# Gate and value products of four token groups as seven half products, and attention numerators scaled in PSUM

## The chip, the core and the metric

The kernel runs on one core of a Trainium2 chip. A core has a matrix engine (TensorE, PE in the profile; its weight loads are shown as PEld), a vector engine (VectorE, DVE), a scalar engine (ScalarE, ACT), a general engine (GpSimd, POOL) and a sync engine (SP) that issues DMAs here. TensorE writes its results to PSUM, which this kernel uses as eight banks of 128 partitions x 512 fp32 values; ACT and DVE take them out; POOL works on SBUF alone in this kernel. Each engine runs its own instructions in the order of the program and waits on semaphores for the others. The metric is the device time of one execution in microseconds (us), lower is better.

## What is computed

A linear attention with an exponential feature map, followed by a gated feed-forward network (FFN):

```python
def phi(x):
    proj = np.einsum('bhsd,df->bhsf', x, w_phi)
    proj = proj - np.max(np.abs(proj), axis=-1, keepdims=True)
    return np.concatenate([np.exp(proj), np.exp(-proj)], axis=-1)
q_p, k_p = phi(q), phi(k)
kv  = np.einsum('bhsf,bhsd->bhfd', k_p, v);  z = np.sum(k_p, axis=2)
num = np.einsum('bhsf,bhfd->bhsd', q_p, kv)
den = np.einsum('bhsf,bhf->bhs', q_p, z)[..., None] + 1e-06
x   = (num / den)                      # to 4608 tokens x 512
out = (np.maximum(x @ w_gate, 0) * (x @ w_val)) @ w_out
```

There are 8 batches, 8 heads, 576 positions and a head size of 64; the FFN goes from 512 to 1536 and back to 512.

## The kernel before

**Tiles.** The first 512 positions of batch b form token group b (0 to 7), in four tiles of 128 tokens; the last 64 positions of all eight batches form group 8. A group's attention result, transposed, is `xT(g)`: four blocks of 128 rows (the 512 inputs of the FFN) by 512 tokens.

**Attention, numerators.** For each tile TensorE makes, per head, the product of the query features with the key-value sums for the two signs s of the exponential (`do_nu`, L899; 65 columns, of which the last is the denominator). The sum over the two signs has to be weighted: the s=1 part is multiplied by a factor per token and head (`cq`, or `cm` for group 8). The heads are taken in three parts of 2, 3 and 3 (`GROUPS`); a bank holds both signs of a part. VectorE then multiplies the s=1 part into an SBUF tile t (`do_nt`, L922), adds the s=0 part into u (`do_nv`, L932), takes the reciprocal of the denominators (`do_nr`, L942), and POOL multiplies u by it to the bf16 tile xu (`do_nx`, L954). A DMA transpose or TensorE turns xu into `xT`.

**FFN, first product.** `do_fv` and `do_fg` (through `ffn_in`, L1078) make a block of 128 of the 1536 value or gate columns for a group's 512 tokens: four matmuls of 128x512 that accumulate in one bank. The value block is copied out as bf16 `val` by ACT (`do_va`, L1096) or DVE (`do_vb`, L1099), and DVE makes h = max(gate, 0) * val (`do_ga`, L1102). Group 0 is done by 128-token tiles instead (L1110).

**FFN, second product.** Groups 1 to 8 already use a Strassen-like scheme (Winograd's form): h and `w_out` are cut in 2 x 2 blocks, and seven half products (`do_fw`, L1247, 12 matmuls of 256 columns each) take the place of eight. The sums of h blocks that it needs are made by POOL (`do_ps`) or DVE (`do_ds`), both L1223, 24 per group; the sums of weights once by POOL (`do_tw`, L1203). The partial results are put together on their way out: ACT copies two banks to SBUF (`do_ys`, L1272, and `do_y2`, L1275), and DVE adds to them in five more steps (`do_yw`, `do_yz`, `do_y1`, `do_y3`, `do_y4`, all L1278).

**Order.** Nothing is scheduled automatically. A string `ORDER` lists all steps (2239 words) in one sequence, each word with the step's name, its arguments, the PSUM banks after a colon and the ring buffers that it takes after an @. A step `x` calls `do_x`, which emits its instructions on their engines; so the sequence fixes each engine's order. Words `zz.n` are n dummy matmuls.

Of the kernel before, what the change touches and what calls it, by code (L numbers as in the profile page):

```python
# [28 lines left out]
vd.0.0.0:2@vs1 qz.0.0:3@my1 vs.0.1.1 qe.0.1.1.1:5 vp.0:2 qu.0.1@mz0 ke.0.2.1.0:6 qe.0.1.1.0:5 wl.0.0
vz.0:2 qb.0.2:4 zz.2:7 qb.1.3:3 zz.2:7 qb.1.2:1 vd.0.0.1:2 qu.0.0@mz1 vz.1:2 qe.0.1.3.0:3@qp2  # L30
vo.2@vs2 qw.0.0@cq0 qx.0.0.3:0 qx.0.0.2:4 qe.0.0.0.0:2 vs.0.2.1 zz.7:7 kv.0.0:6 qx.0.1.3:3 lw.1.1
vs.0.2.0 kc.0.0:6@kv0 kt.1.1@kT3 qe.0.0.0.1:2 kv.0.2:5 kv.0.1:6 qe.0.0.2.1:4@qp3 lm.1.1 kc.0.2:5
wl.1.1 kc.0.1:6 nu.0.0.0:2 nt.0.0.0:2@t0 zz.1:7 nu.0.0.2:5 qw.0.1 qx.0.1.2:1 qe.0.0.2.0:4
qe.0.1.3.1:3 nu.0.0.1:6 nv.0.0.0:2@u0 zz.2:7 nu.0.1.2:4 lv.1.2 nu.0.1.0:2 qe.0.1.2.1:1 nt.0.0.1:6@t1
lm.1.0 nt.0.0.2:5@t2 qy.0.2:3 nv.0.0.1:6 qe.0.0.3.0:0 nv.0.0.2:5 nt.0.1.0:2@t3 zz.2:7 nu.0.1.1:6
qy.0.3:5 nr.0.0@r0 qe.0.1.2.0:1 qz.0.2:3@my2 nv.0.1.0:2@u1 qz.0.3:5@my0 qu.0.2@mz2 zz.5:7
kr.1.1:3125 qe.0.0.3.1:0 nt.0.1.2:4@t0 nt.0.1.1:6@t1 qw.0.2 wl.1.0 nu.0.2.2:0 nx.0.0@xu0 nv.0.1.2:4
xp.0.0:7 nv.0.1.1:6 nt.0.2.2:0@t2 ke.1.1.3.1:5@kp3 nr.0.1@r1 nu.0.2.1:4 xa.0.0:7 nt.0.2.1:4@t3
nu.0.2.0:6 ke.1.1.0.1:3 nt.0.2.0:6@t0 qu.0.3@mz1 ke.1.1.0.0:3 pv.1.0:7 nv.0.2.1:4@u2 nv.0.2.2:0
nv.0.2.0:6 nu.0.3.1:4 qw.0.3 ke.1.1.1.0:1 nx.0.1@xu1 kx.1.1.0:3@mk3 xp.0.1:0 pa.1.0:7@val0  # L40
# [233 lines left out]
def kernel(  # L274
# [679 lines left out]
    def do_nx(bk, b, i):  # L954
        normalize(nc.gpsimd, b, i)
# [408 lines left out]
```

## Time and profile before

| what | value |
|---|---|
| device time, three runs | 366.55, 367.17, 368.11 us (median 367.17) |
| span of the profiled execution, first to last instruction | 365.2 us, granted TensorE clock 0.997 |
| instructions | 10031 |
| DMA traffic | 38.14 MB, mean 104 GB/s |

The profiled execution's own device time is not listed apart from its span; the median lies 1.97 us above that span. In the profile's lines a group of instructions is given as line, engine, operation, out<-in, shapes and count, then busy time in us and the mean of one in ns, then the idle time of the engine just before them with what ended it. In the timeline the columns are start in us, duration in us, engine, line and operation. A matmul's record includes its way through the array, so records of neighbours overlap.

### The profile page before, as it was taken

The numbers are of one execution on the slowest core, as the hardware profiler recorded it, in microseconds if no ns is written. First come the engines' busy times: TensorE is split into PE (matmuls) and PEld (weight loads), VectorE is DVE, ScalarE is ACT, GpSimd is POOL, SyncE is SP. The second block draws the span as 40 slices with busy tenths as digits, with TensorE's granted clock in tenths as the row PEclk, the third lists the DMA queues.
The fourth block names the chain that finished last, engine by engine and source line by source line (L and its number), as shares of the span: only waits on it lengthen the run. The fifth ranks groups of instructions, "written<-read, shape, count | busy, mean of one in ns | idle before, by whom it ended". The sixth has DMA issues, their size and how long they took to land.

```text
span 365.2 us, 10031 instructions
## 1 busy us (share of the span) xinstructions
PE 356.6 (98%) x3900; PEld 224.4 (61%) x3900; DVE 308.1 (84%) x723; ACT 228.8 (63%) x550; POOL 275.8 (76%) x337
## 2 busy tenths in 40 slices
PE   8999999999999999999999999999999999999993
PEld 6579865445575647755676456755457765545682
DVE  5999999989999998989988989899676945448872
ACT  4999996986698768695975278748854221121200
POOL 8765988999999999968997589946975793016600
PEclk9999999999999999999999999999999999999998
DMA  8999999983746893298219660397000320203016
GB/s 128 254 205 206 176 196 143 181 132 53 131 96 131 103 156 71 58 149 109 61 63 126 130 130 0 61 177 137 0 16 2 131 45 0 72 3 115 2 33 197
DMA packets 90768, 38.14 MB, mean 104 GB/s; under 512 B 64226, under 2 KB 86370, under 8 KB 90722
## 3 DMA queue, kind: packets, MB, share of 16 engines
q0 software_dynamic: 33504, 15.03, 32.5%
q1 hardware_dynamic: 56754, 21.83, 27.7%
q10 hardware_dynamic: 464, 0.66, 0.8%
q8 instruction: 30, 0.49, 0.6%
q14 instruction: 16, 0.13, 0.1%
HBM read 37.81 MB, written 9.44 MB: 129 GB/s over the span
## 4 chain that ended last, share of the span: by engine, by line
PE 81%; DVE 9%; POOL 4%; issue 2%; DMA 1%; ACT 1%; SPq 0%; DVEq 0%; POOLq 0%
PE bank L1081 42%; PE bank L1247 18%; PE bank L781 4%; PE bank L1110 4%; PE bank L904 3%; PE bank L1142 2%; PE bank L841 2%; PE bank L579 2%; POOL vs L1223 2%; DVE t L925 1%; DVE h L1102 1%; DVE u L935 1%; DMA w64f<-in_w_phi_dram 1%; ACT kp L675 1%; PE bank L442 1%
## 5 line engine op out<-in xcount | busy, mean ns | idle before, releaser
L675 ACT ACTIVATE kp<-bank 128x384 bf16<-128x384 f32 x192 | 84.1, 513 | 12.8 <-PE bank L579 6.0
L1081 PE MATMUL bank<-xTs,wv 128*128 128x512 bf16 x352 | 87.3, 379 | 0.0
L1096 ACT CAST val<-bank 128x512 bf16<-128x512 f32 x81 | 47.4, 592 | 62.8 <-PE bank L1081 55.7
L1081 PE MATMUL bank<-xTs,wg 128*128 128x512 bf16 x352 | 86.4, 379 | 0.0
L1102 DVE SCALAR_TENSOR_TENSOR h<-bank,val 128x512 bf16<-128x512 f32 x88 | 59.0, 681 | 22.1 <-PE bank L1081 15.0
L856 ACT ACTIVATE qp<-bank 128x512 bf16<-128x512 f32 x128 | 69.8, 619 | 5.3 <-PE bank L841 2.6
L1081 PEld LDWEIGHTS <-wg 128*128 128x128 bf16 x400 | 37.2, 98 | 41.0 <-issue 2.2
L1081 PEld LDWEIGHTS <-wv 128*128 128x128 bf16 x400 | 37.1, 98 | 38.0 <-DMA xTs<-xu 0.4
L732 POOL TENSOR_TENSOR vs<-vn,ek 128x780 bf16<-128x780 f32 (+2 forms) x40 | 53.9, 1364 | 1.2 <-ACT ek L692 0.7
L947 POOL TENSOR_TENSOR xu<-u,r 128x512 bf16<-128x512 f32 x36 | 37.3, 1044 | 16.8 <-DVE r L943 16.6
L683 DVE TENSOR_REDUCE mk<-bank 128x3 f32<-128x384 f32 x96 | 49.1, 542 | 1.0 <-ACT kp L675 0.9
L1247 PEld LDWEIGHTS <-h 128*128 128x128 bf16 x420 | 39.9, 98 | 9.5 <-issue 2.4
L1223 POOL TENSOR_TENSOR vs<-h 128x256 bf16<-128x256 bf16 x42 | 28.0, 670 | 21.4 <-DVE h L1102 14.4
L864 DVE TRANSPOSE_TENSOR_REDUCE maxq<-bank 128x16 f32<-128x512 f32 x56 | 37.1, 691 | 0.4 <-PE bank L841 0.2
L935 DVE TENSOR_TENSOR u<-bank,t 128x195 f32<-128x195 f32 (+1 forms) x108 | 32.7, 327 | 0.7
L925 DVE TENSOR_TENSOR t<-bank,cq 128x195 f32<-128x195 f32 (+1 forms) x96 | 29.4, 325 | 2.0 <-PE bank L904 1.7
L1247 PE MATMUL bank<-wo,h 128*128 128x256 bf16 x252 | 31.0, 273 | 0.0
L904 PEld LDWEIGHTS <-qp 128*128 128x128 bf16 x512 | 23.2, 98 | 10.8 <-issue 1.2
L1223 POOL TENSOR_TENSOR vs<-vs,h 128x256 bf16<-128x256 bf16 x42 | 27.9, 673 | 1.0 <-PE bank L1247 0.2
L904 PE MATMUL bank<-kv,qp 128*128 128x65 bf16 x512 | 26.1, 193 | 0.4 <-DVE u L935 0.2
L1223 POOL TENSOR_TENSOR h<-h 128x256 bf16<-128x256 bf16 x36 | 23.7, 670 | 0.3
L1223 POOL TENSOR_TENSOR h<-h,vs 128x256 bf16<-128x256 bf16 x36 | 23.7, 671 | 0.0
(134 smaller groups left out, 577.3 us busy)
## 6 DMA issues: line engine op xcount, KB each, us to landing
vn<-in_v_dram SPq DMA_DIRECT2D x24, 256.0 KB, 5.5
out_dram<-xTs SPq DMA_DIRECT2D x17, 256.0 KB, 2.4
kn<-in_k_dram POOLq DMA_DIRECT2D x7, 512.0 KB, 8.6
qn<-in_q_dram POOLq DMA_DIRECT2D x7, 512.0 KB, 8.0
out_dram<-obp SPq DMA_DIRECT2D x14, 256.0 KB, 2.4
wv<-in_moe_w_val_dram POOLq DMA_DIRECT2D x3, 512.0 KB, 8.9
wg<-in_moe_w_gate_dram POOLq DMA_DIRECT2D x3, 512.0 KB, 9.3
wo<-in_moe_w_out_dram POOLq DMA_DIRECT2D x3, 512.0 KB, 8.2
```

The source lines that it names most:

```text
L675: nc.scalar.activation(kp_of(3 * b + j)[:, i, s].rearrange("p n f -> p (n f)"), bank[bk[0]][:, 0 : 3 * F], AF.Exp, scale=(1.0, -1.0)[s],)
L683: nc.vector.tensor_reduce(mk_of(3 * b + j)[:, :, i], bank[bk[0]][:, 0 : 3 * F].rearrange("p (n f) -> p n f", f=F), axis=AX.X, op=ALU.max, ...
L732: nc.gpsimd.tensor_tensor(vs_of(3 * b + j)[:, s, 0:n].rearrange("p n i e -> p (n i) e")[:, :, 0:e], src[:, lo:hi].rearrange("p h i e -> p ...
L856: nc.scalar.activation(qp_of(4 * b + i)[:, s, 4 * hq : 4 * hq + 4].rearrange("p h m -> p (h m)"), bank[bk[0]], AF.Exp, scale=(1.0, -1.0)[s],)
L864: nc.vector.tensor_reduce((maxq0[:, i] if b == 0 else maxq)[:, :, i, 4 * hq : 4 * hq + 4].rearrange("p t h -> p h t"), bank[bk[0]].rearran ...
L904: nc.tensor.matmul(bank[bk[0]][:, E * n : E * (n + 1)], lhsT=qp_of(4 * b + i)[:, s, h, :], rhs=kv_of(b)[:, h, s, 0:E],)
L947: eng.tensor_tensor(xu_of(n).rearrange("p (h d) -> p h d", d=D), u_of(n)[:, :, 0:D], r_of(n).to_broadcast([P, H, D]), op=ALU.mult,)
L1081: nc.tensor.matmul(bank[bk[0]], lhsT=w[:, dc, P * f : P * f + P], rhs=xT(g)[:, dc, :], start=(dc == 0), stop=(dc == NDC - 1),)
L1096: nc.scalar.copy(val_of(NFC * g + f), bank[bk[0]])
L1102: nc.vector.scalar_tensor_tensor(h2_of(g, f), bank[bk[0]], 0.0, val_of(NFC * g + f), op0=ALU.max, op1=ALU.mult)
L1223: eng.tensor_tensor(sum_of(g, n, j), a, b, op=op)
L1247: nc.tensor.matmul(bank[bk[0]][:, col : col + HN], lhsT=x[:, P * u : P * (u + 1)], rhs=w, start=(n in (1, 5, 6) and u == us[0] and j == 0) ...
```

## The change

Four things change together.

**First product of groups 5, 6 and 8, 7.** They are taken in two pairs. The inputs (512) are cut in two halves, upper and lower; for a block f of 128 columns the four results wanted are gate and value of the first group of a pair and gate and value of the second. With x1, x2 the halves of the first group's `xT`, x3, x4 those of the second's, and G, V the gate and value weights (upper u, lower l), seven half products of two matmuls each (`do_fi`) are made:

```
S1 = Vu - Gu   S2 = Vl - S1   S3 = Vl - Vu   S4 = Gl - S2     (weights, once)
T1 = x3 + x4   T2 = T1 - x1   T3 = x1 - x3   T4 = x2 - T2     (tokens, per pair)
M1 = Gu x1   M2 = Gl x2   M3 = Vl T4   M4 = S4 x4   M5 = S1 T1   M6 = S2 T2   M7 = S3 T3
gate, first = M1+M2          value, first  = M1+M6+M5+M3
gate, second = M1+M6+M7+M4   value, second = M1+M6+M7+M5
```

The sums are seeded by copies: ACT copies the bank with M1 to a second bank (`do_ia`), M6 accumulates onto that copy, ACT copies the result to a third (`do_ib`), and M2, M7, M3 and M4 accumulate in place. M5 is copied to an SBUF tile qs by ACT (`do_iq`) or DVE (`do_ir`); DVE adds it to a bank to give the bf16 `val` (`do_iv`, twice per block), and M4 may only accumulate after the second of these has read its bank. `do_ga` is as before. The weight sums are 24 steps of 128x512 bf16 (22 on POOL, 2 on DVE), the token sums 16 (9 on POOL, 7 on DVE).

**Second product.** The same seeding takes the place of part of the adds: `do_fa` and `do_fb` copy one bank to another on ACT, later half products accumulate there, and fewer adds are left for DVE (15 of 128x512 and 2 of 128x256, against 38 and 4).

**Numerators.** The heads are taken in two halves of four. `do_nu` makes the s=1 part first; DVE multiplies it by the factor in place in PSUM (`do_nt`); a second `do_nu` accumulates the s=0 part on it; DVE takes the reciprocals from PSUM (`do_nr`, 4 columns) and writes xu from PSUM (`do_nx`). The tiles t and u and POOL's step are gone; TensorE's matmuls are as many as before.

**Order.** A new `ORDER` of 2386 words; 85 dummy matmuls as before. The number of buffers for h grows from 16 to 18, and group 6 and half of group 7 keep h in other tiles that are free by then.

```diff
-    GROUPS = HEADS
+    HALVES = ((0, 4), (4, 8))
...
     def do_nt(bk, b, i, g):
-        lo, hi = GROUPS[g]
-        n = hi - lo
+        lo, hi = HALVES[g]
         nc.vector.tensor_tensor(
-            t_of(3 * serial(b, i) + g)[:, 0:n],
-            parts(bk, n)[:, :, 1],
-            scales(b, i)[:, lo:hi][:, :, None].to_broadcast([P, n, E]),
+            part(bk, g),
+            part(bk, g),
+            scales(b, i)[:, lo:hi][:, :, None].to_broadcast([P, hi - lo, E]),
             op=ALU.mult,
         )
...
+    def do_fi(bk, p, f, n):
...
+        for dc in range(2):
+            nc.tensor.matmul(
+                bank[bk[0]],
+                lhsT=w[:, dc, P * f : P * f + P],
+                rhs=x[:, dc, :],
+                start=(n in (1, 5) and dc == 0),
+                stop=(dc == 1),
+                skip_group_check=(n not in (1, 5)),
+            )
+
+    def do_ia(bk, p, f):
+        nc.scalar.copy(bank[bk[1]], bank[bk[0]])
+
+    def do_ib(bk, p, f):
+        nc.scalar.copy(bank[bk[1]], bank[bk[0]])
+
+    def do_iq(bk, p, f):
+        nc.scalar.copy(qs_of(("in", p, f)), bank[bk[0]])
...
+    def do_iv(bk, p, f, u):
+        nc.vector.tensor_tensor(
+            val_of(NFC * PAIRS[p][u] + f), bank[bk[0]], qs_of(("in", p, f)), op=ALU.add
+        )
...
+    def do_fa(bk, g):
+        nc.scalar.copy(bank[bk[1]], bank[bk[0]])
```

The new order moves work on every engine; three places show what the prediction speaks of.

VectorE, numerators of group 4, before (lines of `before`: L925 is t, L935 is u, L943 the reciprocal, L1102 makes h):

```order
L925 TENSOR_TENSOR t_126<-bank_66,cq_115 128x195
L935 TENSOR_TENSOR u_127<-bank_66,t_126 128x195
L925 TENSOR_TENSOR t_123<-bank_67,cq_115 128x195
L935 TENSOR_TENSOR u_127<-bank_67,t_123 128x195
L1102 SCALAR_TENSOR_TENSOR h_152<-bank_68,val_143 128x512
L925 TENSOR_TENSOR t_125<-bank_69,cq_115 128x130
```

and now (L949 scales in place, L958 the reciprocal, L962 writes xu, L1000 and L1101 are a transpose and h):

```order
L949 TENSOR_TENSOR bank_66<-bank_66,cq_115 128x260
L949 TENSOR_TENSOR bank_69<-bank_69,cq_115 128x260
L1000 STREAM_TRANSPOSE qt_130<-qm_74 128x256
L1101 SCALAR_TENSOR_TENSOR h_148<-bank_70,val_137 128x512
L958 RECIPROCAL r_124<-bank_69 128x4
L958 RECIPROCAL r_123<-bank_66 128x4
L962 TENSOR_TENSOR xu_128<-bank_66,r_123 128x256
L962 TENSOR_TENSOR xu_126<-bank_69,r_124 128x256
```

Three pairs of steps per tile have become two triples, and between the first and the second of a triple TensorE has a part to add.

TensorE, block 5 of the second pair (groups 8 and 7), now; bank0 receives M1 of block 5, and bank5 is the copy of it that M6 accumulates on (xTm is `xT(8)`, the tiles kp, qT, qr and vn hold sums of weights and tokens):

```order
L1180 MATMUL bank0_63<-xTm_147,wg_143 128x512
L1180 LDWEIGHTS kp_2_83
L1180 MATMUL bank7_70<-xTs_146,kp_2_83 128x512
L1180 LDWEIGHTS kp_2_83
L1180 MATMUL bank7_70<-xTs_146,kp_2_83 128x512
L1180 LDWEIGHTS wv_144
L1180 MATMUL bank2_65<-qr_0_131,wv_144 128x512
L1180 LDWEIGHTS wv_144
L1180 MATMUL bank2_65<-qr_0_131,wv_144 128x512
L1180 LDWEIGHTS kp_0_81
L1180 MATMUL bank5_68<-qT_0_107,kp_0_81 128x512
```

Two half products of other blocks (bank7 and bank2) stand between the product that is copied and the one that needs the copy; before, no TensorE instruction of the FFN's first product needed anything of ACT or DVE beyond `xT` and a free bank.

SP, the end of its queue, before (L1304, L1308 and L1300 write results of groups 8, 7 and 7):

```order
L1304 DMA out_dram<-obp 64x512 x2
L1308 DMA out_dram<-xTs 128x2x256
L1304 DMA out_dram<-obp 64x512 x2
L1308 DMA out_dram<-xTs 128x2x256 x2
L1300 DMA out_dram<-xTs 128x256
```

and now (L1429, L1421 and L1425 write results of groups 7, 7 and 8):

```order
L1429 DMA out_dram<-xTs 128x2x256 x2
L1421 DMA out_dram<-xTs 128x256
L1425 DMA out_dram<-obp 64x512 x4
```

Four DMAs of group 8's half tiles, which wait for the last half product of all, have become the last of the queue; before, it was one DMA.

743 lines of the change are left out of this document (414 added, 329 removed).

## Prediction

> **What bounds the kernel now.** I read the page's first part, then busy time by stretch, then the chain that ended last, then who waited for whom.
>
> ```profile
> PE 356.6 (98%) x3900; PEld 224.4 (61%) x3900; DVE 308.1 (84%) x723; ACT 228.8 (63%) x550; POOL 275.8 (76%) x337
> ```
>
> ```profile
> 0.00:220.00 220.00, 217.36 (x2687) 138.18 (x2688) 206.30 (x501) 171.28 (x423) 193.60 (x230) 1.00 0.84 132
> 220.00:300.00 80.00, 79.99 (x841) 49.70 (x840) 62.99 (x151) 47.77 (x111) 63.63 (x81) 1.00 0.35 65
> 300.00:360.00 60.00, 59.23 (x376) 36.49 (x373) 38.85 (x72) 9.75 (x18) 18.57 (x28) 1.00 0.17 50
> ```
>
> The columns are the stretch, its length, busy time of PE, PEld, DVE, ACT and POOL, the granted clock, the DMA share and GB/s. PE is never free after the start. VectorE is at 94% up to 220 us and has 17.0 + 21.2 = 38.2 us free after that.
>
> A busy PE might hide waits, since records overlap; the chain and the waits tell:
>
> ```profile
> PE 81%; DVE 9%; POOL 4%; issue 2%; DMA 1%; ACT 1%; SPq 0%; DVEq 0%; POOLq 0%
> ```
>
> ```profile
> 316.71 13.81 PE bank L1081 x64
> 331.84 10.36 PE bank L1081 x48
> 342.20 17.05 PE bank L1247 x156
> ```
>
> ```profile
> PE bank L904 <- DVE u L935: 0.2, 1, 0.2
> PE bank L904 <- ACT kv L792: 0.2, 1, 0.2
> PE bank L1247 <- DVE obp L1278: 0.2, 1, 0.2
> ```
>
> Matmuls of the first product follow one another at 13.81/64 = 0.216 us, those of the second at 17.05/156 = 0.109 us, and after the start nothing holds PE for more than 0.2 us at a time. So PE's own work sets the time, and taking PE work away pays in full unless a wait comes in its place.
>
> **The change, part by part.**
>
> *PE.* A pair's block took 2 groups x 2 products x 4 = 16 matmuls and now takes 7 x 2 = 14. Over 2 pairs x 12 blocks that is 48 matmuls of 128x512 fewer: 48 x 0.216 = **-10.4 us**. The numerators keep their matmuls (16 of 65 columns a tile, now in two visits), and so does the second product.
>
> *VectorE.* The rows:
>
> ```profile
> L1102 DVE SCALAR_TENSOR_TENSOR h<-bank,val 128x512 bf16<-128x512 f32 x88 | 59.0, 681 | 22.1 <-PE bank L1081 15.0 <-ACT val L1096 5.1 <-PE bank L1247 1.1
> L935 DVE TENSOR_TENSOR u<-bank,t 128x195 f32<-128x195 f32 x72 | 24.3, 352 | 0.7
> L925 DVE TENSOR_TENSOR t<-bank,cq 128x195 f32<-128x195 f32 x64 | 21.4, 345 | 1.3 <-PE bank L904 1.1
> L935 DVE TENSOR_TENSOR u<-bank,t 128x130 f32<-128x130 f32 x36 | 10.0, 278 | 0.1
> L1278 DVE TENSOR_TENSOR obp<-bank,obp 128x512 f32<-128x512 f32 x21 | 14.2, 681 | 4.3 <-PE bank L1247 4.3
> L1278 DVE TENSOR_TENSOR xTs<-bank,xTs 128x256 f32<-128x256 f32 x4 | 1.7, 424 | 0.3 <-PE bank L1247 0.2
> L943 DVE RECIPROCAL r<-u 128x8 f32<-128x8 f32 x36 | 6.6, 189 | 0.2
> L1223 DVE TENSOR_TENSOR kp<-kp 128x256 bf16<-128x256 bf16 x6 | 3.1, 515 | 0.0
> L1223 DVE TENSOR_TENSOR kp<-kp,vs 128x256 bf16<-128x256 bf16 x6 | 1.6, 281 | 0.0
> ```
>
> A tile's numerator took 2 x (0.345 + 0.352) + 2 x 0.28 + 0.19 = 2.14 us of VectorE. Now it takes two steps that scale in place, two that write xu, and two reciprocals. No row shows VectorE writing to PSUM. From below the bound is the 195-column row, 0.345; from above a whole bank, 0.681. A step of 256 columns that reads PSUM takes 0.424, and I take 0.42 for both: 2 x (0.42 + 0.42 + 0.19) = 2.06, or 36 x 0.08 = 3 us less in all. Then 48 adds that make val: + 48 x 0.68 = 32.7; M5 copied by VectorE 7 times: + 4.8; 18 value copies fewer: - 12.3 (the whole-bank price); the second product's adds, 23 of 0.68 and 2 of 0.42 fewer and 5 copies more: - 13.1; 20 sums of h more, at 0.28 to 0.52, say 0.43: + 8.6; 9 sums of 128x512, bounded by 0.28 and twice 0.52, say 0.55: + 5. Together about +23, so 331 us of busy time in a span near 357, or 93%.
>
> Does this fit? The numerators keep the stretch to 220 us as full as it is. The first products of groups 5 to 8 come after that, where 38 us are free and some 32 us (32.7 + 4.8 + 8.6 + 5 - half of 12.3 - half of 13.1) are added, while the stretch loses 10 us. By records it is just too much. But records overlap in a dense queue:
>
> ```profile
> 327.98 1.29 DVE L1102 SCALAR_TENSOR_TENSOR h<-bank,val 128x512 bf16<-128x512 f32 x2 [1.66 <-PE bank L1081]
> ```
>
> Two whole-bank steps of 0.69 take 1.29, so the second starts 0.60 after the first. A block of a pair needs 2 adds and 2 h steps, 4 x 0.60 = 2.4 us, in the 14 x 0.216 = 3.0 us that PE spends on it. VectorE stays behind PE's work, with some 15% to spare in the densest stage.
>
> *ScalarE.* It gains 63 whole copies from bank to bank, 2 halves, and 23 copies to qs, and loses 30 value copies and 3 others:
>
> ```profile
> L1096 ACT CAST val<-bank 128x512 bf16<-128x512 f32 x81 | 47.4, 592 | 62.8 <-PE bank L1081 55.7 <-DVE h L1102 5.2 <-DVE u L935 0.6
> L1151 ACT COPY obp<-bank 128x512 f32<-128x512 f32 x2 | 1.3, 673 | 0.0
> L703 ACT ACTIVATE bank<-mk 128x12 f32<-128x12 f32 x2 | 0.4, 180 | 0.0
> ```
>
> At 0.59 this is +33 us, 262 of 357: no bound by itself. What matters is the delay of a copy, because PE now waits for it. From the end of the chain of matmuls:
>
> ```profile
> 352.51 1.47 PE L1247 MATMUL bank<-kp,kp 128*128 128x256 bf16 x12
> 353.82 0.82 PE L1247 MATMUL bank<-wo,vs 128*128 128x256 bf16 x6
> 354.02 1.22 DVE L1278 TENSOR_TENSOR xTs<-bank,xTs 128x512 f32<-128x512 f32 x2 [0.42 <-PE bank L1247]
> ```
>
> PE was free at 353.82, and the reader of its bank started at 354.02: 0.20 us. With the same 0.04 between the record's end (353.98) and the reader taken for the way back, a seed costs 0.20 + 0.59 + 0.04 = 0.83 us from PE to PE. Counted in the new order at the rows' prices, the nearest use of a seed stands two half products later, 4 x 0.216 = 0.86, in 10 of 48 places, and 0.79 in one; the rest have 0.98 or more. So at the row's price it is covered, and the queue on ACT has to be free at that moment. The in-place step has 0.20 + 0.42 + 0.04 = 0.66; six of the 72 parts have less than that between their two visits (0.39 to 0.59), which is 1.0 us in sum. Bounds for all these waits: nothing, and 4.1 us for a seed of 1.15 (a copy of 0.91). I take **+1.0 us**. The two small rows on a bank of 12 columns let me expect no dearer copy: L703, which writes PSUM, has 0.18. The Trainium skill's "PSUM — Partial Sum Buffer" (Specifications, the engine access table) says that ScalarE writes faster to PSUM than to SBUF; by that a seed would be below 0.83 and the sum 0.1 us less, and no row here shows it for a whole bank.
>
> *POOL.* It loses 36 steps of 1.04 and 26 sums of 0.67, and gains 31 sums of 128x512:
>
> ```profile
> L947 POOL TENSOR_TENSOR xu<-u,r 128x512 bf16<-128x512 f32 x36 | 37.3, 1044 | 16.8 <-DVE r L943 16.6
> L1223 POOL TENSOR_TENSOR vs<-h 128x256 bf16<-128x256 bf16 x42 | 28.0, 670 | 21.4 <-DVE h L1102 14.4 <-PE bank L781 5.3 <-DMA xTm<-xu 1.5
> L1203 POOL TENSOR_TENSOR kp<-wo 128x768 bf16<-128x768 bf16 x4 | 6.6, 1647 | 0.0
> ```
>
> Half way between 0.67 and 1.65 is 1.16; 31 of them make 36 us, so the total falls by some 19 us to 257. But 22 weight sums (25 us) stand close together behind the last key scaling of group 7, because they use tiles that only then are free, and the first pair needs them third by third. PE's first pair takes 36 us for its 12 blocks, and the first third is needed at once. Bounds: hidden, and 4 of these sums late, 4.6 us. I take **+0.5 us**, near the lower end, since the order puts PE's work on group 7's queries and numerators in front.
>
> *The end.*
>
> ```profile
> 357.75 1.47 PE L1247 MATMUL bank<-wo,kp 128*128 128x256 bf16 x12
> 359.64 0.94 ACTq L1323 DMA_DIRECT2D out_dram<-xTs  x1
> 359.71 0.34 SPq L1300 DMA_DIRECT2D out_dram<-xTs  x1
> 355.32 1.15 SPq L1304 DMA_DIRECT2D out_dram<-obp  x2
> out_dram<-xTs ACTq DMA_DIRECT2D x1, 128.0 KB, 4.6
> out_dram<-obp SPq DMA_DIRECT2D x4, 128.0 KB, 2.4
> ```
>
> PE is free at 359.06 (12 x 0.109 after 357.75), the last DMA starts 0.65 later and lands after 4.6, behind others. Now a whole-bank copy comes after the last matmul (0.20 + 0.59 + 0.05 = 0.84), and four DMAs at 1.15/2 = 0.58 each, so the last starts at 2.6. If it lands after 2.4 the end comes 0.2 us earlier than before; after 4.6, 2.0 us later. I take the middle, **+0.9 us**.
>
> *Sum.* 365.2 - 10.4 + 1.0 + 0.5 + 0.9 = 357.2 us of span. The profiled execution's span is 1.97 below the median of the runs shown (367.17), so the forecast is **359.2 us**; by the parts' own bounds 356.9 (no waits, landing after 2.4) to 367.
>
> **The rivals.**
>
> *VectorE in bursts: 364.* 331 us of records and the 10 us that it cannot use (the start, and the last 6 us) leave 16 of 357. If the sums of h share their time with POOL's (0.52 against 0.28 in two rows of one shape) and val comes late, PE waits for a bank. 44 sums x 0.12 more is 5 us. For it speaks the 94% up to 220 us; against it that PE hardly waits there now.
>
> *The in-place step costs two passes, slower: 373.* One mechanism: reading and writing one bank, VectorE takes as long as for t and u together, 0.83 us for 260 columns, by the two rows of 195. That adds 72 x 0.41 = 30, so VectorE needs 361 + 10, and the span ends at 371. The point from which it decides is 16/72 = 0.22 more than 0.42, so 0.64 us. Nothing here shows a VectorE write to PSUM; against it speaks that t and u take the same for different outputs.
>
> *Seeds are slow: 369.* A bank-to-bank copy of twice 0.59 makes a seed of 1.42; 29 of the 48 places have 1.31 or less behind them, and what they lack sums to 10 us. That is the gain given back. For it: no row shows a whole-bank copy into PSUM; against it: the rows of ACT's whole-bank copies lie between 0.59 and 0.67 whatever they write.
>
> *POOL's weight sums are late: 363,* by the 4.6 above.
>
> *The clock falls: 366.* PE would stop briefly at many seeds, and a lower clock would double its steps, as at the start:
>
> ```profile
> 1.06 3.38 PE L442 MATMUL bank<-zero 128*128 128x256 bf16 x15 [1.06 <-DVE zero L428]
> 15.51 0.94 PE L442 MATMUL bank<-zero 128*128 128x256 bf16 x7
> ```
>
> (3.38 - 0.42)/14 = 0.21 us each there, (0.94 - 0.27)/6 = 0.11 later. If a tenth of the 336 half-product matmuls ran so, 34 x 0.216 = 7 us. Against it: the clock stands at 1.00 in all three stretches. The Trainium skill's "TensorE: Matmul & The Clock Gate" (A second HAM failure mode: psum-queue depth-cycling) speaks for this rival: it reports a kernel that cycled through PSUM banks at 512 columns and whose short idles between groups made the clock go down and up. This trace, with eight banks in turn and no such idles, does not show it.
>
> **How the numbers follow.** Chances: the forecast 0.62, VectorE in bursts 0.09, POOL late 0.08, two passes 0.13, slow seeds 0.05, clock 0.03. About 0.5%, 1.8 us, is what a measurement of this kernel can tell from no change. Faster takes the forecast, the two late cases: 0.79; same takes the slow seeds and the clock: 0.08; slower takes the two passes: 0.13. The range leaves out the two passes and the worst of the seeds above, and little below: 355.5 to 368; the forecast's own range is 356.5 to 362.
>
> **What would show it.** Right: some 48 fewer matmuls of 128x512, PE's records without gaps to the end, PE's first and last matmul about 10 us closer, VectorE near 330 us, clock 1.00. Each step: L949 at about 0.42 (over 0.64 is the slower case); bank-to-bank copies near 0.59 (1.18 is the slow seed); waits of PE on DVE in the numerators, on ACT and POOL in the half products of the first product; the last copy at 0.8 and the last DMA 2.6 us after PE's end. It is wrong if PE shows waits of over 5 us in sum, whoever is named.

## The result and the profile after

The changed kernel takes 387.45 us (median of five runs, 383.83 to 393.64), the kernel before 367.20 (366.55 to 368.11) beside it: a ratio of 1.053, 95% interval 1.0475 to 1.0587. One of the five runs, 393.64, is in a slower state, and the ratio is that of the other four. The kernel is slower by 20 us where 8 us less were forecast. The profiled execution took 389.48 us, with a span of 387.7 us.

The page of the changed kernel, engines, clock in 40 slices, and the chain that ended last:

```profile
PE 359.4 (93%) x3852; PEld 225.8 (58%) x3852; DVE 339.0 (87%) x736; ACT 254.8 (66%) x608; POOL 259.6 (67%) x306
PEclk9988899999999998799999999999999999999998
PE 58%; POOL 13%; DVE 12%; DMA 8%; SPq 3%; issue 2%; ACT 1%; POOLq 0%; DVEq 0%; ACTq 0%
```

The 48 matmuls are gone (3900 to 3852). But TensorE's share of the chain fell from 81% to 58%, that of POOL rose from 4% to 13%, that of the DMAs from 1% to 8% and that of SP's queue from 0 to 3%, and the clock sags in slices 3 to 5 and in 16 and 17.

Busy time by stretch (columns as in the prediction), first the kernel before, then the changed one:

```profile
0.00:60.00 60.00, 57.84 (x862) 42.88 (x866) 55.62 (x143) 50.90 (x130) 47.24 (x61) 1.00 1.19 189
100.00:160.00 60.00, 59.73 (x727) 38.43 (x724) 57.21 (x133) 48.53 (x120) 57.62 (x70) 1.00 0.59 106
240.00:280.00 40.00, 39.99 (x330) 21.78 (x327) 31.62 (x68) 26.85 (x63) 28.87 (x35) 1.00 0.40 67
```

```profile
0.00:60.00 60.00, 52.13 (x710) 40.51 (x711) 47.16 (x108) 43.75 (x107) 34.80 (x47) 0.91 1.15 185
100.00:160.00 60.00, 51.07 (x544) 29.57 (x541) 48.71 (x105) 42.48 (x106) 43.99 (x51) 0.91 0.61 101
240.00:280.00 40.00, 37.58 (x461) 23.51 (x459) 39.80 (x94) 28.90 (x69) 39.13 (x40) 1.00 0.21 48
```

In the first two stretches every engine is busy less, VectorE too, at 0.91 of the clock (POOL also has the 36 steps to xu less to do). When all engines idle more, either a load is late or the engines wait for each other in turn; the waits have to tell which. Neither stretch holds a pair's first product, which starts at 262.4 us, but both hold the new numerators. The waits of the changed kernel (us in total, times, longest):

```profile
POOL vr L782 <- DMA vm<-in_v_dram: 16.6, 2, 12.6
PEld L1210 <- DMA wg<-in_moe_w_gate_dram: 3.0, 1, 3.0
PE bank L803 <- POOL vs L754: 4.3, 2, 3.7
PE bank L1347 <- DVE vs L1323: 5.1, 2, 3.6
PE bank L1180 <- DVE qT L1152: 1.2, 1, 1.2
PE bank L1180 <- POOL kp L1125: 0.5, 1, 0.5
ACT bank L1190 <- PE bank L1180: 13.9, 11, 2.9
```

All waits of PE that the profile lists add up to 21.8 us, after 2.4 in the kernel before, and before, no step of POOL waits for vm. By the prediction's own sign (over 5 us of such waits) it is wrong.

The largest loss can be followed through three timelines (start, duration, engine, line), of SP's queue, of POOL, of PE:

```profile
130.95 8.06 SPq L540 DMA_DIRECT2D vn<-in_v_dram  x4
139.06 4.18 SPq L1421 DMA_DIRECT2D out_dram<-obp  x1
143.28 0.63 SPq L559 DMA_DIRECT2D vm<-in_v_dram  x1
```

```profile
133.78 0.94 POOL L505 DMA_DIRECT2D qn<-in_q_dram  x1
147.34 1.05 POOL L782 TENSOR_TENSOR vr<-vm,ek 64x520 bf16<-64x520 f32 x1 [12.61 <-DMA vm<-in_v_dram]
149.13 1.50 POOL L754 TENSOR_TENSOR vs<-vn,ek 128x780 bf16<-128x780 f32 x1
```

```profile
152.70 0.38 PE L803 MATMUL bank<-vs,kp 128*128 128x65 bf16 x4 [3.69 <-POOL vs L754]
```

In the new order the small load of batch 4 (the last 64 rows of v, 64 KB, tile vm) stands on SP's queue behind the four loads of vn and an output. The five took 12.2 us to issue. POOL's next step reads vm, so POOL stood for 12.6 us; the scalings of the values behind it were late, and PE waited for them, with a lower clock after it.

Another stop of PE, of nearly the same size, has VectorE's name. At 110.92 us VectorE began a sum of h that took 4.29 us, while POOL ran its own steps one behind the other:

```profile
110.92 4.29 DVE L1323 TENSOR_TENSOR vs<-h 128x256 bf16<-128x256 bf16 x1
115.28 2.53 PE L1347 MATMUL bank<-wo,vs 128*128 128x256 bf16 x11 [3.58 <-DVE vs L1323]
```

All other sums of this shape take 0.28 to 1.13 us. POOL had come to this place after a wait of 4.0 us for batch 3's vm, at 98 to 102. In e2_vm below, where only loads of vm move, the same sum takes 0.46 us and this wait of PE is gone. So late loads can stand behind a wait that names an engine; why the sum took so long at this place is not shown.

To see what each stretch lost I took, for every matmul of the trace, the time to the start of the next, less what its kind takes where nothing holds it (the lower quartile of its kind after 60 us in the two first traces); dummy matmuls count as loss. Matmuls that a later trace lacks (45) are put in at their kind's price. This is worked out, not a view of the profile. PE's work at undisturbed prices is 314.4 us before and 304.0 us after, 10.4 less. PE's loss:

| stretch, us | before | changed | e3_both | e6_v4 | e13_v2 | e14_light | e16_order |
|---|---|---|---|---|---|---|---|
| 0 to 60 | 20.3 | 29.5 | 25.6 | 25.3 | 23.3 | 23.3 | 29.2 |
| 60 to 100 | 5.0 | 5.2 | 5.0 | 5.0 | 5.3 | 5.3 | 5.1 |
| 100 to 160 | 7.5 | 19.3 | 15.2 | 11.5 | 10.3 | 9.7 | 20.0 |
| 160 to 240 | 7.3 | 9.0 | 9.0 | 9.4 | 10.7 | 9.9 | 8.5 |
| 240 to 280 | 3.1 | 9.6 | 7.6 | 6.7 | 5.9 | 3.3 | 6.9 |
| 280 to end | 0.9 | 4.2 | 4.2 | 4.2 | 4.1 | 3.9 | 4.1 |
| sum | 44.1 | 76.9 | 66.7 | 62.2 | 59.7 | 55.3 | 73.9 |

So -10.4 of work and +32.8 of loss make the +22.4 of span. 21 of the 32.8 lie in the stretches 0 to 60 and 100 to 160.

### The profile page after: what moved, and what is told of

Its sections match the earlier page's. It is cut to its first block, busy times and chain, and to the rows that moved or that the text cites. A ratio compares the mean times of both kernels' runs of the same rounds, so it can differ in the third digit from the quotient of the medians.

```text
span 387.7 us, 10020 instructions
## 1 busy us (share of the span) xinstructions
PE 359.4 (93%) x3852; PEld 225.8 (58%) x3852; DVE 339.0 (87%) x736; ACT 254.8 (66%) x608; POOL 259.6 (67%) x306
## 3 DMA queue, kind: packets, MB, share of 16 engines
q0 software_dynamic: 33504, 15.03, 29.8%
## 4 chain that ended last, share of the span: by engine, by line
PE 58%; POOL 13%; DVE 12%; DMA 8%; SPq 3%; issue 2%; ACT 1%; POOLq 0%; DVEq 0%; ACTq 0%
PE bank L1080 15%; PE bank L1180 14%; PE bank L1347 9%; DMA wg<-in_moe_w_gate_dram 4%; PE bank L1210 4%; POOL vs L754 3%; PE bank L803 3%; DMA vm<-in_v_dram 3%; PE bank L1242 3%; PE bank L464 2%; PE bank L925 2%; DVE vs L1323 2%; SPq L540 2%; PE bank L601 2%; POOL vs L1323 2%
## 5 line engine op out<-in xcount | busy, mean ns | idle before, releaser
L1101 DVE SCALAR_TENSOR_TENSOR h<-bank,val 128x512 bf16<-128x512 f32 x82 | 55.2, 678 | 4.5 <-PE bank L1080 2.7
L754 POOL TENSOR_TENSOR vs<-vn,ek 128x780 bf16<-128x780 f32 (+2 forms) x40 | 54.0, 1360 | 3.1 <-ACT ek L714 2.7
L1080 PE MATMUL bank<-xTs,wv 128*128 128x512 bf16 x208 | 53.2, 389 | 0.0
L1080 PE MATMUL bank<-xTs,wg 128*128 128x512 bf16 x208 | 52.0, 382 | 0.9 <-DVE h L1101 0.9
L1323 POOL TENSOR_TENSOR vs<-h 128x256 bf16<-128x256 bf16 x31 | 20.6, 669 | 43.6 <-DVE h L1101 43.0
L1347 PEld LDWEIGHTS <-h 128*128 128x128 bf16 x396 | 38.0, 98 | 8.2 <-DVE h L1323 0.9
L1095 ACT CAST val<-bank 128x512 bf16<-128x512 f32 x51 | 30.5, 619 | 13.7 <-PE bank L1080 12.0
L1202 DVE TENSOR_TENSOR val<-bank,qs 128x512 bf16<-128x512 f32 x48 | 31.8, 680 | 7.9 <-PE bank L1180 4.7
L925 PEld LDWEIGHTS <-qp 128*128 128x128 bf16 x512 | 25.7, 100 | 14.4 <-issue 3.0
L782 POOL TENSOR_TENSOR vr<-vm,ek 64x520 bf16<-64x520 f32 x14 | 14.8, 1055 | 25.2 <-DMA vm<-in_v_dram 16.6
L1080 PEld LDWEIGHTS <-wg 128*128 128x128 bf16 x208 | 18.4, 98 | 21.4 <-issue 4.7
L1080 PEld LDWEIGHTS <-wv 128*128 128x128 bf16 x208 | 19.1, 99 | 19.8 <-issue 2.3
L1347 PE MATMUL bank<-wo,h 128*128 128x256 bf16 x240 | 29.7, 274 | 0.3 <-DVE h L1323 0.3
L925 PE MATMUL bank<-kv,qp 128*128 128x65 bf16 x512 | 29.1, 197 | 0.8 <-ACT kv L814 0.6
L949 DVE TENSOR_TENSOR bank<-bank,cq 128x260 f32<-128x260 f32 x64 | 25.9, 424 | 4.1 <-PE bank L925 4.0
L962 DVE TENSOR_TENSOR xu<-bank,r 128x256 bf16<-128x256 f32 x72 | 28.1, 410 | 0.2
L1190 ACT COPY bank<-bank 128x512 f32<-128x512 f32 x24 | 13.8, 573 | 20.9 <-PE bank L1180 13.9
L803 PEld LDWEIGHTS <-kp 128*128 128x128 bf16 x640 | 22.3, 98 | 8.7 <-issue 5.3
```

The lines of the kernel that those rows point to most:

```text
L754: nc.gpsimd.tensor_tensor(vs_of(3 * b + j)[:, s, 0:n].rearrange("p n i e -> p (n i) e")[:, :, 0:e], src[:, lo:hi].rearrange("p h i e -> p ...
L803: nc.tensor.matmul(out_ps[:, h - lo, s, :], lhsT=lhsT, rhs=rhs, start=(at == 0), stop=(at == 2 * n * (C + 1) - 1),)
L925: nc.tensor.matmul(bank[bk[0]][:, E * n : E * (n + 1)], lhsT=qp_of(4 * b + i)[:, s, h, :], rhs=kv_of(b)[:, h, s, 0:E], start=(s == 1 and h ...
L1080: nc.tensor.matmul(bank[bk[0]], lhsT=w[:, dc, P * f : P * f + P], rhs=xT(g)[:, dc, :], start=(dc == 0), stop=(dc == NDC - 1),)
L1101: nc.vector.scalar_tensor_tensor(h2_of(g, f), bank[bk[0]], 0.0, val_of(NFC * g + f), op0=ALU.max, op1=ALU.mult)
L1323: eng.tensor_tensor(sum_of(g, n, j), a, b, op=op)
```

## The experiments

Theory: the new order's places in the queues of DMAs and of POOL lose the time, and the new arithmetic gives its 10.4 us. Rival: the new arithmetic's helpers (seeding copies, in-place scaling, weight sums) lose it. A word of `ORDER` such as `wl.1.0` is a load of a third of the gate weights, `wo.i` of the output weights, `lv.b.i` of a quarter of batch b's values (vn), `lw.b.h` of half of the small tile vm, `vq` and `vs` are POOL's scalings of vm and vn. All ratios are to the kernel before, measured beside each run, with the 95% interval; where the intervals of two rows overlap (the changed kernel's is 1.0475 to 1.0587), their difference is no more than a hint:

| run | median, us | ratio |
|---|---|---|
| e1_start | 384.17 | 1.046 (1.042 to 1.050) |
| e2_vm | 381.30 | 1.037 (1.035 to 1.040) |
| e3_both | 379.31 | 1.033 (1.029 to 1.036) |
| e4_noseed | 389.40 | 1.058 (1.053 to 1.062) |
| e5_fill | 379.01 | 1.033 (1.027 to 1.038) |
| e6_v4 | 376.11 | 1.023 (1.020 to 1.026) |
| e7_wsum | 377.64 | 1.028 (1.026 to 1.030) |
| e8_fill_v4 | 377.73 | 1.025 (1.020 to 1.030) |
| e9_giveback | 384.28 | 1.045 (1.042 to 1.048) |
| e10_noscale | 375.00 | 1.020 (1.017 to 1.023) |
| e11_best | 374.39 | 1.018 (1.016 to 1.020) |
| e12_before_late | 374.57 | 1.019 (1.017 to 1.021) |
| e13_v2 | 373.54 | 1.017 (1.015 to 1.018) |
| e14_light | 367.81 | 1.001 (1.000 to 1.003) |
| e15_lighter | 368.34 | 1.002 (1.000 to 1.004) |
| e16_order | 384.62 | 1.047 (1.042 to 1.051) |

**Loads re-ordered.** e1_start, in the order of the words:

```diff
-wo.1
+wl.1.0
+wl.1.1
...
-wl.1.0
-wl.1.1
...
 wl.1.2
+wo.1
...
-lv.2.3
-lv.2.2
 lv.1.3
 lv.1.2
 lv.1.0
-lv.2.1
 lw.1.1
 lv.1.1
+lv.2.3
+lv.2.2
+lv.2.1
```

> The changed kernel with only its early loads re-ordered: two thirds of the gate weights are issued ahead of the first third of the output weights, and three value loads of batch 2 behind the last value load of batch 1. Nothing else moves. Theory (the places in the load queues cost the time): in the changed kernel PE is busy 52.1 of the first 60 us, in the kernel before 57.8, and the first gate product waits until 38.3 us for its weights; with the loads in the order of need that wait goes, PE is busy 56 us or more of the first 60, and the time falls by 5 to 8 us, to 380 to 382. Rival (the new arithmetic, its hops between ScalarE, VectorE and PE, costs the time): PE's start gets better, but what is gained is lost again behind it, 386 to 388.

e2_vm:

```diff
 vq.2.0
+lw.3.1
+lw.3.0
...
-lw.3.0
-lw.3.1
...
+lw.4.1
 lw.4.0
...
 lv.4.2
-lw.4.1
 vq.4.1
```

> The changed kernel with only three small loads re-ordered on SP's queue: the rows of v beyond 512 for batch 3 (both halves) stand right behind the POOL step that frees their tile, and those of batch 4 (second half) stand beside the first half, ahead of four value loads and an output. Nothing else moves. Theory (places in the queues): POOL's waits for this tile, 4.0 us at 98 to 102 and 12.6 us at 135 to 147, go; PE's lost time in 100 to 120 (3.6 us idle, clock 0.91) and 140 to 160 (5.4 us idle, clock 0.83) goes with them, and the time falls by 9 to 13 us, to 375 to 379. Rival (the new arithmetic): POOL's waits go, PE's idle time in these stretches stays, under another name (DVE or ACT), 385 to 388.

e3_both is both edits.

> The changed kernel with both re-orderings, the early loads and the three small loads. Theory (places in the queues): the two gains add, 14 to 20 us, so 367 to 373, what is left over 359 being the waits for the weight sums on POOL (3.3 us at 260 to 280), for the sums of h near 300 to 320 (2.5 us) and near the end. Rival (the new arithmetic): 383 to 388.

e1 gained 3.3 us of the 5 to 8 expected, e2 6.2 of 9 to 13, both together 8.1 of 14 to 20. None fits its rival (386, 385 and 383 or more), and the theory had the sizes wrong; behind vm's delay stood a second one. In e3_both POOL no longer waits for vm, but 11.0 us for the loads of vn, which may only start when batch 3's last scaling has freed their tile:

```profile
POOL vs L754 <- DMA vn<-in_v_dram: 11.5, 2, 11.0
```

**The seeds left out.** e4_noseed, with `ia` and `ib` taken out of the order:

```diff
-                start=(n in (1, 5) and dc == 0),
+                start=(n in (1, 3, 5, 6) and dc == 0),
```

> The changed kernel without the 48 bank-to-bank copies of the pairs' first product: the half products that would start on a copied sum start on an empty bank, so that h of the four groups lacks these sums. All else, the order of the loads too, is as in the changed kernel. Theory (places in the queues): PE's waits at the seeds are under 1 us in sum, so the time stays, 385 to 388. Rival (the seeds cost the time: PE waits at the hops, the clock follows): most of the 20 us come back, 366 to 372.

389.40: nothing comes back. The rival falls for the seeds, as the waits said: no row of PE names ACT's copies, and ACT waits for PE.

**What stands behind.** e5_fill took fillers out of the first 20 us of e3_both's order (29 of them, not the 33 that the expectation names):

```diff
 zz.6:3
-zz.6:4
...
-zz.2:0
 zz.2:1
-zz.2:2
-zz.2:3
-zz.2:4
-zz.2:0
-zz.2:1
...
```

> The kernel with both re-orderings, and of the filler matmuls on the zero tile, which stand on PE's queue in the first 20 us, 33 of 68 taken out (in the new order they stand closer together and ahead of work that could start). Theory (places in the queues): PE reaches the first key transposes and features 2 to 3 us earlier, and the 7 us by which the first 40 us do less work than before shrink to 2 to 4; time 375 to 377.5 after 379.3. Rival: PE waits there for data anyway, and without the fillers the granted clock falls, 379 to 382.

379.01, the same as e3_both: here the rival held. PE was ready for its first gate product at 31.1 us (33.8 in e6_v4, 34.9 in e3_both) and then waited for the weights; the DMA engines are full until 60 us (share 1.19 and 1.15 in the first stretch of the two kernels above):

```profile
PE bank L1209 <- DMA wg<-in_moe_w_gate_dram: 3.2, 1, 3.2
```

e6_v4 freed batch 3's tile earlier and put batch 4's loads ahead of two outputs (the words' old places are left out here):

```diff
 kk.3.2.0
+kk.3.2.1
+vs.3.2.0
+vs.3.0.0
+vs.3.2.1
 ps.1.3.4
...
+lv.4.1
+lv.4.3
+lv.4.0
+lv.4.2
 od.0.0
...
```

> The kernel with both re-orderings, and batch 4's value loads (which wait until the last scaling of batch 3's values on POOL has freed their tile) earlier: the last three of these scalings stand ahead of three sums of h on POOL, one exponential on ACT stands earlier, and the four loads stand ahead of two outputs on SP. Theory (places in the queues): POOL's wait of 11.0 us for these loads at 128 to 139 shrinks to 4 to 6, and PE's loss in 140 to 160 (6.8 us in place of 2.4) with it, 375 to 377 after 379.3. Rival (the new arithmetic): PE's loss there stays, 379.

376.11, within the expectation. SP's queue and the middle stretch of e6_v4:

```profile
116.49 2.74 SPq L540 DMA_DIRECT2D vn<-in_v_dram  x4
```

```profile
100.00:160.00 60.00, 55.62 (x714) 36.13 (x723) 55.23 (x125) 49.24 (x121) 51.68 (x65) 1.00 0.71 113
```

The four loads go out at 116.49, not at 130.95, and in 2.74 us; the clock is back at 1.00, and PE's loss in 140 to 160 fell from 6.8 to 3.3. Three sums of h that were passed over are now late for PE (3.0 us at 115), so 1.8 us came back in 100 to 120.

e7_wsum makes three of the four weight sums on an eighth of their columns:

```diff
-        cols = slice(SF * third, SF * (third + 1))
+        cols = slice(SF * third, SF * third + (SF if n == 1 else 64))
```

> The kernel with both re-orderings, and three of the four weight sums of the pairs' first product made on 64 of 512 columns of each third (the rest is left as it was, so h of the pairs' groups is off): some 16 us of POOL's work are gone from 250 to 277, all places stay. Theory (POOL's weight sums come late): PE's loss of 7.6 us in 240 to 280, of which the kernel before has 3.1, goes to 3 to 4, and the time falls by 3.5 to 4.5 us, to 375 to 376. Rival (VectorE is the bound there, at 19.9 of 20 us): the loss stays, 378 to 380.

377.64, 1.7 us below e3_both, between the two, and the intervals just overlap: POOL's weight sums cost at most about 2 of the 4.5 us that 240 to 280 loses against before.

e8_fill_v4 joined e5's and e6's edits.

> The edits of e5_fill and of e6_v4 together. Theory (places in the queues): the gains add, 371 to 375. Rival (the new arithmetic): 379 or more.

377.73, not 371 to 375: the fillers' removal gives nothing here either. In this profile PE still waits for the gate weights, now 1.3 us.

**Is the saving real, and what do the helpers cost?** e9_giveback gives e6_v4 48 matmuls with zero weights:

```diff
+            if n == 4:
+                nc.tensor.matmul(
+                    bank[bk[0]],
+                    lhsT=zero[:, 0:P],
+                    rhs=x[:, dc, :],
+                    start=False,
+                    stop=(dc == 1),
+                    skip_group_check=True,
+                )
```

> The kernel of e6_v4, with the 48 matmuls of 128x512 that the half products save given back: each fourth half product of a pair issues two more matmuls with zero weights into its bank (same result, same order, same loads). Theory (the saving is real, 10.4 us, and what is lost is lost elsewhere): these 48 cost 0.216 us each, so the time rises by 8 to 10.4 us, from 376.1 to 384 to 386.5. Rival (PE waits in the pairs' first product anyway, for seeds, VectorE or POOL): the matmuls fall into these waits, 376 to 380.

384.28, 8.2 us more than e6_v4: the saved matmuls are worth 0.17 us each in the end, four fifths of the 0.216 forecast. PE does bind for most of the pairs' first product.

e10_noscale takes every `nt` out of e6_v4's order:

```diff
 nu.0.0.1.1:7
-nt.0.0.1:7
 nu.0.0.1.0:7
...
```

> The kernel of e6_v4 without the steps that scale half of the numerator in its bank (72 steps of 0.42 us on VectorE left out, so the two halves of the numerator are summed unscaled). All else is in place. Theory (places in the queues; the step costs what its row shows): VectorE falls from 335 to some 307 us, PE's remaining losses stay for the most part, and the time falls by 1 to 4 us, 372 to 375. Rival (VectorE, at 90%, is the bound and sends PE waiting in bursts): the time falls by 8 us or more, 368 or less.

375.00: VectorE fell from 335.0 to 314.4 us of busy time and the kernel by 1.1, with overlapping intervals. In this order VectorE's load was not what sent PE waiting, for the most part.

**The converse.** e12_before_late leaves the kernel before as it is and makes one load late:

```diff
+wo.1
+wo.2
 wl.1.1
...
 wl.1.0
...
-wo.1
...
-wo.2
```

> The kernel before, with its old arithmetic and its old order, and only two loads moved: two thirds of the output weights (512 KB each) are issued ahead of the two thirds of the gate weights that the first products read. Theory (a load behind others in a queue costs its whole delay, whatever the arithmetic): the gate weights land some 5 us later and the first gate product waits, so the time rises by 3 to 6 us, to 370 to 373. Rival (the old order takes such a delay): 367 to 368.

374.57, 7.05 us slower than before (367.52), more than expected. The old arithmetic loses a third of the change's loss by two words:

```profile
PE bank L1110 <- DMA wg<-in_moe_w_gate_dram: 4.8, 1, 4.8
```

**How far the order goes.** e11_best is e6_v4 with e5's fillers out, `wl.1.1` (which the first gate product reads) ahead of `wl.1.0`, and two sums of h ahead of the last two scalings:

```diff
+wl.1.1
 wl.1.0
-wl.1.1
...
 vs.3.2.0
+ps.1.3.4
+ps.1.3.1
 vs.3.0.0
 vs.3.2.1
-ps.1.3.4
-ps.1.3.1
```

> The kernel of e6_v4 with three places changed further: the filler matmuls of e5_fill taken out; the gate weights' second third, which the first gate product reads, issued ahead of the first third; two sums of h ahead of the last two value scalings of batch 3 on POOL. In e5_fill PE came 2.7 us earlier to its first gate product and then waited 3.2 us for that load. Theory (places in the queues): that wait goes and the gain at the start stays (2 to 3 us), PE's wait of 3.0 us for a sum of h at 115 goes, so 370 to 373. Rival (the next bound stands right behind): 375 to 377.

374.39, between theory and rival. e13_v2 then puts batch 2's value loads behind a load that waits:

```diff
-lv.2.3
-lv.2.2
-lv.2.1
...
 lw.2.1
+lv.2.3
+lv.2.2
+lv.2.1
 lv.2.0
```

> The kernel of e11_best with three value loads of batch 2 (256 KB each) behind the small load that waits for batch 1's POOL steps at 49 us, so that they no longer stand ahead of batch 2's keys in the full DMA queues of the first 60 us. Theory (order of the loads): VectorE's wait of 2.5 us for these keys at 50 to 53 and PE's loss of 5.3 us in 40 to 60 (before 2.0) shrink by 2 to 3 us, 371.5 to 373. Rival (other loads fill the queues as well): 374 to 375.

373.54, a little above the expected range, and its interval overlaps that of e11_best; PE's loss in 40 to 60 fell from 5.3 to 2.7. This is the fastest complete version found, 1.7% slower than the kernel before.

e14_light is e13_v2 without what e7 and e10 leave out, e15_lighter also without what e4 leaves out.

> The kernel of e13_v2 without the in-place scaling steps (half of each numerator left unscaled) and with three of the four weight sums on 64 of 512 columns: VectorE has some 27 us and POOL some 16 us less to do. Theory now (order first, and of the rest a small part is the helpers' load: e10_noscale gained 1.1 us, e7_wsum 1.7): 3 us less than e13_v2, 368.5 to 370. Rival (what remains is the load of VectorE and POOL): 10 us less or more, 362 or below.

> The kernel of e14_light, and the 48 seeding copies left out too. Theory: the seeds are covered, so no more than 1 us less than e14_light. Rival (the seeds matter once the other waits are gone): 3 us less or more.

367.81 and 368.34. The helpers' load is worth 5.7 us once the order no longer hides it, twice what I expected and half of what the rival did; the seeds are worth nothing again. The stretch 240 to 280, e13_v2 and then e14_light:

```profile
240.00:280.00 40.00, 36.81 (x308) 19.41 (x313) 38.68 (x84) 22.61 (x49) 32.99 (x30) 1.00 0.20 54
```

```profile
240.00:280.00 40.00, 38.84 (x296) 20.01 (x300) 36.24 (x79) 22.89 (x50) 20.13 (x33) 1.00 0.19 52
```

With the helpers PE is free 3.2 us there while VectorE is at 97%; without them 1.2 us. (These traces lack 45 matmul records, so both are upper values.)

e16_order is the decisive one: the changed kernel's own order, and none of the three helpers. The half products, the 48 adds to val, the sums of tokens and the second product's new copies are still there.

> The changed kernel with its own order, every place as it was, and without the new helper steps: no seeding copies, no in-place scaling, three of four weight sums on 64 of 512 columns (the output is off by what is left out). Theory (the order's places in the queues lose the time): it stays at 383 to 387, above the kernel before by 15 us or more, though 43 us of helper work are gone. Rival (the new arithmetic's helpers lose it): 370 or less.

```profile
0.00:60.00 60.00, 52.04 (x717) 40.26 (x720) 44.88 (x101) 43.98 (x109) 34.77 (x47) 0.91 1.16 187
100.00:160.00 60.00, 49.63 (x527) 29.27 (x534) 45.72 (x92) 41.22 (x104) 42.67 (x50) 0.91 0.59 98
```

384.62: 2.8 us of the 20 come back, with overlapping intervals. The two stretches look as in the changed kernel, clock included, and so do the waits (L767, L1195, L788, L739, L1332 and L1308 are the lines that were L782, L1210, L803, L754, L1347 and L1323):

```profile
POOL vr L767 <- DMA vm<-in_v_dram: 12.9, 1, 12.9
PEld L1195 <- DMA wg<-in_moe_w_gate_dram: 3.0, 1, 3.0
PE bank L788 <- POOL vs L739: 5.1, 2, 4.4
PE bank L1332 <- DVE vs L1308: 5.4, 2, 3.8
```

So in this order the time is lost without the three helpers too. Edits of the order alone, 29 dummy matmuls fewer among them, gave back 13.9 us (387.45 to 373.54).

## Why the prediction was wrong

Step by step, as the prediction put it.

- **PE -10.4: right.** 304.0 us of work after 314.4, and 8.2 us when given back.
- **The prices: right.** The groups of the changed kernel (line, operation, shapes, count, busy time and mean ns):

```profile
L949 DVE TENSOR_TENSOR bank<-bank,cq 128x260 f32<-128x260 f32 x64 | 25.9, 424 | 4.1 <-PE bank L925 4.0
L962 DVE TENSOR_TENSOR xu<-bank,r 128x256 bf16<-128x256 f32 x72 | 28.1, 410 | 0.2
L1190 ACT COPY bank<-bank 128x512 f32<-128x512 f32 x24 | 13.8, 573 | 20.9 <-PE bank L1180 13.9 <-DVE qs L1199 3.0 <-DVE val L1202 1.4
L1196 ACT COPY qs<-bank 128x512 f32<-128x512 f32 x17 | 9.8, 592 | 6.0 <-PE bank L1180 4.0 <-DVE kp L1101 1.4 <-DVE val L1202 0.6
L1202 DVE TENSOR_TENSOR val<-bank,qs 128x512 bf16<-128x512 f32 x48 | 31.8, 680 | 7.9 <-PE bank L1180 4.7 <-ACT qs L1196 3.0
L1125 POOL TENSOR_TENSOR kp<-wv,vn 128x512 bf16<-128x512 bf16 x6 | 7.0, 1181 | 0.0
```

  Scaling in place 0.424 (0.42 taken), xu 0.410 (0.42), a seed's copy 0.573 (0.59), val 0.68 (0.68), a weight sum 1.18 (1.16). So the rivals of two passes and of slow seeds fall. The Trainium skill's "PSUM — Partial Sum Buffer" (Specifications, the engine access table) has ScalarE faster to PSUM than to SBUF: 573 against 592 ns (L1190 and L1196) agrees, and it changes nothing.
- **VectorE 331, ACT 262, POOL 257:** 339.0, 254.8 and 259.6. VectorE's 8 us more are its sums: those of h (L1323) take it 29.8 us in all, where 10.4 from before and 8.6 more were reckoned (last section), and the nine of 128x512 take 8.0 where 5 were.
- **Waits +1.0 at seeds and numerators:** no wait of PE on ACT's copies is listed, and none on the scaling; e4 and e15 gained nothing. Right in substance.
- **POOL's weight sums +0.5 (0 to 4.6):** mis-sized. PE's waits in the pairs' first product for sums of weights and tokens add to 2.8 us (1.2, 0.5, 0.4, 0.4 and 0.3; two of them stand above), and e7 gained 1.7; the scaling steps and these sums together 5.7 in e14.
- **VectorE in bursts, a rival at 364:** in part. Its cause, sums of h that take longer beside POOL, did occur, and PE waited 5.1 us in two places for such sums; but one of them, 3.6 us, is the place at 111 to 115 us that went with the loads of vm in e2_vm.
- **The end +0.9:** too much; from the start of PE's last matmul to the span's end it is 6.35 us, after 6.29 before.
- **The clock:** as a rival it was to fall at the half products. It is 1.00 in 240 to 280, where they begin, and falls in 0 to 60 and 100 to 160, where PE stops for loads, POOL and VectorE. The mode that "TensorE: Matmul & The Clock Gate" of the Trainium skill (A second HAM failure mode: psum-queue depth-cycling) describes is not seen.
- **The range by the parts' own bounds:** its lower end comes to 356.6 by the terms given (365.2 - 10.4 - 0.2 + 1.97), not 356.9; it changes nothing.

**The step that failed is the sum itself.** It had terms for what the change adds and removes and none for what the new order moves. It took over from the kernel before that "after the start nothing holds PE for more than 0.2 us at a time" and let PE waits arise only where the new arithmetic puts them. But the order was new on every queue: gate weights behind a third of the output weights and beside batch 2's values, vm behind five DMAs on SP, the last scalings of batch 3 behind sums of h. In its place the runs showed waits for loads: POOL 12.6 us for vm and PE 2.9 us for the gate weights, 21.0 us more loss in 0 to 60 and 100 to 160, and 13.9 us back by edits of the order alone. The rows to see this coming stood in the profile of before: DMA engines at a share of 1.19 with 189 GB/s over the first 60 us, vm and vn loads in another order on SP's queue, and POOL, at 57.62 of 60 us in 100 to 160, the engine that both feed. The order of SP and POOL in both kernels was there to be compared, and the prediction compared only SP's last five rows.

What stays open: of the 28.3 us between forecast and result, 13.9 came back by the order and 5.7 by leaving out scaling and weight sums. e14_light, with the order mended by hand and these two left out, is still 8.6 us above 359.2. Its loss stands above that of before by 3.0 us in 0 to 60, 2.2 in 100 to 160, 2.6 in 160 to 240 and 3.0 after 280, in many small pieces. That an order exists in which the half products win was not shown.

## What to carry to other kernels

When a change comes with a new order, price the order before the arithmetic: for each load, what stands ahead of it on its queue, when its tile becomes free, and which in-order engine stands still until it lands. A small load that an engine needs next belongs ahead of large ones that nobody needs yet, and full DMA queues make each load ahead of it count. If all engines idle more in a stretch, ask first for a late load, and follow a wait that names an engine back to what that engine waited for; the same order without the new helper steps (e16) tells the two apart in one run.

## What the runs showed of the hardware

**VectorE's bf16 sums beside POOL.** A sum of two SBUF tiles of 128x256 bf16 takes VectorE 0.278 us alone and mostly some 0.75 while POOL runs one of its own. Rows of the changed kernel, the first from a time in which POOL is idle:

```profile
L1323 DVE TENSOR_TENSOR vs<-vs,qp 128x256 bf16<-128x256 bf16 x3 | 0.8, 278 | 0.0
L1323 DVE TENSOR_TENSOR vs<-vs,kp 128x256 bf16<-128x256 bf16 x3 | 2.2, 751 | 0.0
L1323 POOL TENSOR_TENSOR vs<-vs,kp 128x256 bf16<-128x256 bf16 x3 | 2.1, 699 | 0.0
```

Of 50 such sums of VectorE (the trace, overlap of the records with POOL's), 12 ran alone, at 0.277 to 0.281, and 38 beside POOL, at a median of 0.751 (six of them at 0.28 to 0.29, the longest 4.29); a step that reads a whole bank has 0.68 on the mean in both kernels. Giving VectorE sums to relieve POOL so seems to help little while POOL is busy; no run here tests it. The Trainium skill's "SBUF — State Buffer" (SBUF: two separate sides) has this as a port pair that one of the two holds for a whole instruction while the other waits. The trace agrees for most: 0.75 lies between 0.28 and 0.28 + 0.67, the wait for the rest of POOL's sum in course. The one of 4.29 us ran beside seven steps of POOL, so there the wait was not over with POOL's first.

**The price of issuing.** The same four loads of 256 KB took SP 8.06 us to issue at 130.95 us, while POOL's loads of keys and queries (512 KB each) were under way, and 2.74 us in e6_v4 ahead of them. So issuing has no fixed price on this queue, and what stands behind waits for it. That it grows with what is outstanding fits these two places, and no run tests it alone.

**The clock after a stop.** The changed kernel, 140 to 160 us:

```profile
140.00:160.00 20.00, 14.65 (x123) 7.24 (x120) 11.31 (x27) 10.82 (x26) 12.59 (x14) 0.83 0.51 81
```

PE was idle 5.4 us, its clock fell to 0.83, and its loss was 10.1, 7.7 above before: 2.3 us more than the idle time. The trace has the clock at one half from 152.1 to 159.0 us, right behind the stop, and that this took the 2.3 us is inferred. In 240 to 280 PE was idle 2.4 us in small pieces, and the clock stayed at 1.00.
